# A written-out order of work, rearranged: chunked attention and a sine MLP on one core

## The chip, the core and the metric

The kernel runs on one core of one Trainium2 chip. The metric is the device time of one execution in microseconds. Three executions of the kernel before took 212.36, 212.89 and 215.1 us; the median is 212.89. One further execution was profiled: 213.36 us, of which the traced span is 211.6.

## The reference

Attention over chunks of 32 queries, for 4 batches, 8 heads, 768 positions and head size 64. A chunk's queries see 8 memory rows, the 16 positions to its left, the chunk itself and 8 positions to its right. The result, 3072 tokens of 512 numbers, goes through an MLP whose activation adds a squared sine.

```python
for c in range(nc):                       # chunks of 32
    k_full = np.concatenate([mem_k, k_ctx], axis=2)
    v_full = np.concatenate([mem_v, v_ctx], axis=2)
    scores = scale * np.matmul(q_c, k_full.transpose(0, 1, 3, 2))
    a = np.exp(scores - np.max(scores, axis=-1, keepdims=True))
    a = a / (np.sum(a, axis=-1, keepdims=True) + 1e-09)
    out[:, :, c_start:c_end] = np.matmul(a, v_full)
...
h = x @ w_in                              # 512 -> 2048
s = np.sin(alpha * h)
g = h + s * s / (alpha + 1e-09)
return g @ w_out                          # 2048 -> 512
```

## The kernel before

The program is a chain of five stages. Stage -1 is the attention of batch 0. Stage i (0 to 3) is the MLP of batch i, with the attention of batch i+1 laid into it, so that TensorE always has matmuls to do. A batch's 768 positions are eight blocks of 96 (three chunks each). Each stage's `xT` holds that batch's attention result, transposed, as the input of the next stage's first layer.

No scheduler sets the order. Each stage is a string of words, and `Stage.run` calls one method per word, in the order in which the words stand; each engine then gets its instructions in that order and works through them in order, with semaphores between engines. The words that matter here:

- `bN`, `hN`: first layer of tile N of 16 (128 hidden units), for the first and the second half of the positions, four matmuls each (L460); `h` adds the sine on ScalarE (ACT, L475). The tile holds a pair of PSUM banks.
- `qNV`, `qNA`, `qNP`: the square of tile N's sine on VectorE (DVE), ScalarE or GpSimd (POOL) (L480, L483). `gN`: `h + s*s/alpha` on DVE into `gT` (L487), which frees the pair of banks.
- `oG` opens the second layer of the stage; `fN` lets it do up to N of its 96 matmuls (L498). A finished output tile is copied to SBUF by DVE or ACT in turn (L505) and stored by SP (L508).
- `sABC`: one score group of batch i+1: the scores of blocks A, B, C (L421) and then their exponentials on ACT (L435), each block in a pair of banks. `vA`: its values (L450), normalised on DVE (L394, L395) into one of six `x_blk` buffers.
- `tA`, `TA`: block A is turned into `xT` by four TensorE transposes (L407) and a copy on DVE or ACT (L410). `cA`: the same by a transposing DMA issued by SP (L671), without TensorE.
- `kN`, `lN`, `KN`, `LN`: turns of k and q of batch 1 on TensorE and their copies. Batches 2 and 3 take k and q by rows (`R`, POOL's DMAs L232, L238, L245) and by transposing DMAs on SP (`X`, L260, L263).
- `I`, `U`, `V`, `d`: loads of `w_in`, `w_out`, v, and k or q, issued by POOL (L213, L219, L172 and L179, L155). They stand in POOL's queue between its squares. `W`: a one-element activation that has ACT load a function table.
- In stage -1, `vAB` are the values of head pair A, half B (L380), and `nA`, `yA`, `rA` make the reciprocals of pair A's sums.

TensorE, DVE, ACT and POOL meet in eight PSUM banks. `Banks` gives out, at build time, the pair that was given back longest ago; a tile's first half waits for the earlier reader of the pair's first bank, and its second half for that of the second. The single buffer of `xT` is free by the time the next batch's blocks are written, since all `b` and `h` of a stage come before its first `v`. A block by crossbar and a block by TensorE differ in these lines:

```python
def turn_x(self, a, eng):                     # t, T
    turned(x_blk, x[:, :, QW * int(a):QW * int(a) + QW], eng)
    xslots.give(x_blk)
def do_c(self, a):                            # c
    xslots.give(x_blk, 14)
    nc.sync.dma_start_transpose(x, x_blk[:].rearrange("p g e d -> p (g e d)"))
```

Of the kernel before, what the change touches and what calls it, by code (L numbers as in the profile page):

```python
# [85 lines left out]
def kernel(  # L86
# [769 lines left out]
    def const_a():  # L856
# [13 lines left out]
    ))  # L870
    for i, words in enumerate(((
# [6 lines left out]
    ),(  # L878
# [5 lines left out]
    ),(  # L884
# [5 lines left out]
    ),(  # L890
# [3 lines left out]
    ))):  # L894
        stage = Stage(i, stage.nx).run(words)
    feed.take(400)
# [29 lines left out]
```

## Time and profile before

| what | us |
|---|---|
| median of three executions | 212.89 |
| profiled execution, its own time | 213.36 |
| its traced span | 211.6 |
| TensorE matmul busy | 203.7 (96% of the span) |
| ACT busy | 144.1 (68%) |
| DVE busy | 136.6 (65%) |
| POOL busy | 101.0 (48%) |
| stage 0 and the scores and values in it | 22.8 to 73.8 |
| stage 1 | 73.8 to 120.4 |
| stage 2 | 120.4 to 166.4 |
| stage 3 and the last second layer | 166.4 to 211.6 |

All times in the profile count from the span's start. The granted TensorE clock is 1.00 in every 10 us of it. A matmul's recorded duration overlaps the next one's, so TensorE's own pace is read from the starts, that is, from a chain row's time divided by its count. A row of the chain is start, duration and what was done, with xN for N instructions in a row; a row of the timeline adds the operation's shapes and, in brackets, for how long the engine had waited and for whom.

### The profile page before, as it was taken

To read this page: it belongs to the slowest core of one execution; us is meant where nothing else is said; L and a number is where in the kernel's file an instruction comes from. 1 tells how busy PE (TensorE), PEld (TensorE's weight loads), DVE (VectorE), ACT (ScalarE), POOL (GpSimd) and SP (SyncE) were. 2 spreads that over 40 slices of the span, in tenths; PEclk is the share of its full clock that TensorE was granted. 3 is DMA by queue.
4 is the path that set the end of the run, shared out by engine and by line. 5 is a ranking of instruction groups with operands and counts; after the bars stand their busy time and mean duration, and the time that the engine had idled before them with its cause. 6 is when DMAs were issued, how large, how long until landed. Compare 5 with 4: busy or idle time off the path is not lost.

```text
span 211.6 us, 4427 instructions
## 1 busy us (share of the span) xinstructions
PE 203.7 (96%) x1701; PEld 112.6 (53%) x1701; DVE 136.6 (65%) x219; ACT 144.1 (68%) x229; POOL 101.0 (48%) x132
## 2 busy tenths in 40 slices
PE   7897999999999999999999999999999999999993
PEld 2563565655455555555456555554555565654442
DVE  6773698999362669957675669896347287864011
ACT  4699598967838579978827299878755199991110
POOL 8999608497696390019990058579300022200000
PEclk9999999999999999999999999999999999999999
DMA  6999999999999899969999239959944400000312
GB/s 172 184 155 153 208 206 204 204 155 178 171 162 108 161 138 142 163 101 118 133 232 123 71 87 133 175 104 125 173 114 114 136 3 0 0 5 8 141 51 99
DMA packets 95853, 27.02 MB, mean 128 GB/s; under 512 B 84808, under 2 KB 92376, under 8 KB 95832
## 3 DMA queue, kind: packets, MB, share of 16 engines
q0 software_dynamic: 70240, 14.43, 94.0%
q1 hardware_dynamic: 25376, 12.27, 25.0%
q8 instruction: 13, 0.21, 0.4%
q10 hardware_dynamic: 216, 0.05, 0.1%
q14 instruction: 8, 0.07, 0.1%
HBM read 29.66 MB, written 6.29 MB: 170 GB/s over the span
## 4 chain that ended last, share of the span: by engine, by line
PE 79%; DVE 7%; DMA 4%; POOL 3%; ACT 3%; issue 2%; DVEq 0%
PE ps L498 38%; PE ps L460 32%; DMA vw<-in_v_dram 4%; PE ps L450 3%; DVE gT L487 2%; PE ps L421 2%; PE ps L725 2%; DVE s L483 2%; ACT u L475 1%; ACT s L480 1%; DVE kT L298 1%; PE ps L407 1%; POOL vw L179 1%; POOL s L483 1%; POOL vw L172 1%
## 5 line engine op out<-in xcount | busy, mean ns | idle before, releaser
L498 PE MATMUL ps<-w_out_sb,gT 128*128 128x512 bf16 (+2 forms) x400 | 89.1, 371 | 0.0
L460 PE MATMUL ps<-xT,w_in_sb 128*128 128x384 bf16 x512 | 86.2, 326 | 0.6 <-DVE gT L487 0.4
L487 DVE SCALAR_TENSOR_TENSOR gT<-s,inv_alpha,ps 128x768 bf16<-128x768 f32 x64 | 63.1, 1012 | 12.3 <-ACT s L480 5.3
L475 ACT ACTIVATE u<-ps,alpha_sb 128x768 f32<-128x768 f32 x64 | 56.6, 895 | 18.5 <-PE ps L460 16.0
L460 PEld LDWEIGHTS <-w_in_sb 128*128 128x128 bf16 x512 | 49.8, 98 | 35.6 <-issue 2.4
L498 PEld LDWEIGHTS <-gT 128*128 128x128 bf16 x400 | 36.5, 98 | 37.9 <-DVE gT L487 0.2
L483 POOL TENSOR_TENSOR s<-u 128x768 f32<-128x768 f32 x11 | 17.2, 1567 | 69.2 <-ACT u L475 69.1
L435 ACT ACTIVATE pt<-ps,biasm 128x256 bf16<-128x256 f32 x72 | 27.2, 490 | 10.5 <-PE ps L421 10.5
L505 DVE COPY o_sb<-ps 128x512 f32<-128x512 f32 (+1 forms) x15 | 10.1, 678 | 28.3 <-PE ps L498 26.4
L483 DVE TENSOR_TENSOR s<-u 128x768 f32<-128x768 f32 x23 | 21.9, 953 | 7.3 <-ACT u L475 7.3
L480 ACT ACTIVATE s<-u 128x768 f32<-128x768 f32 x30 | 25.0, 841 | 0.5
L505 ACT COPY o_sb<-ps 128x512 f32<-128x512 f32 (+1 forms) x10 | 5.6, 562 | 21.6 <-PE ps L498 21.6
L395 DVE TENSOR_TENSOR x_blk<-ps,rinv 96x512 bf16<-96x512 f32 x24 | 16.5, 686 | 0.8
L172 POOL DMA_DIRECT2D vw<-in_v_dram x13 | 11.9, 913 | 5.1 <-PE ps L407 5.1
L179 POOL DMA_DIRECT2D vw<-in_v_dram x13 | 13.3, 1020 | 0.4 <-issue 0.4
L394 DVE RECIPROCAL rinv<-ps 96x8 f32<-96x8 f32 x24 | 4.7, 198 | 12.7 <-PE ps L450 12.7
L238 POOL DMA_DIRECT2D kst<-in_k_dram x16 | 11.8, 736 | 2.2 <-DMA vw<-in_v_dram 1.6
L232 POOL DMA_DIRECT2D kst<-in_k_dram x16 | 11.7, 733 | 1.4 <-DMA w_out_sb<-in_moe_w_out_dram 0.7
L245 POOL DMA_DIRECT2D q_bf<-in_q_dram x12 | 10.7, 910 | 0.0
L450 PEld LDWEIGHTS <-pt 128*128 128x128 bf16 x192 | 8.2, 97 | 4.2 <-ACT pt L435 0.3
L725 PE MATMUL ps<-zeros 128*128 128x512 bf16 x19 | 7.8, 489 | 1.3 <-DVE zeros L755 1.3
L450 PE MATMUL ps<-vw,pt 128*128 128x65 bf16 x192 | 8.9, 193 | 0.0
(89 smaller groups left out, 136.0 us busy)
## 6 DMA issues: line engine op xcount, KB each, us to landing
out_dram<-o_sb SPq DMA_DIRECT2D x23, 256.0 KB, 2.7
q_bf<-in_q_dram POOLq DMA_DIRECT2D x12, 128.0 KB, 6.6
w_in_sb<-in_moe_w_in_dram POOLq DMA_DIRECT2D x1, 1152.0 KB, 12.1
vw<-in_v_dram POOLq DMA_DIRECT2D x7, 128.0 KB, 7.2
vw<-in_v_dram POOLq DMA_DIRECT2D x8, 112.0 KB, 7.2
kst<-in_k_dram POOLq DMA_DIRECT2D x14, 64.0 KB, 4.7
kst<-in_k_dram POOLq DMA_DIRECT2D x14, 56.0 KB, 4.5
w_out_sb<-in_moe_w_out_dram POOLq DMA_DIRECT2D x2, 384.0 KB, 9.9
```

What stands on the lines that cost most here:

```text
L172: nc.gpsimd.dma_start(vw[0:64, lo:c1, 0:D], win(vflat, a, n, 64))
L179: nc.gpsimd.dma_start(vw[72:128, c0:hi, 0:D], win(vflat, base + QW * c0 + 48, hi - c0, 56))
L395: nc.vector.tensor_tensor(out=x_blk[:].rearrange("p g e d -> p e g d"), in0=otv[0:QW, :, :, 0:D], in1=rinv[:].unsqueeze(3).to_broadcast([Q ...
L435: nc.scalar.activation(pt[:, 0:H * QW].rearrange("p (g e c) -> p g e c", g=2, e=4)[:, :, :, 32 * m:32 * m + 32], sc[:, :, 0:4 * QW].rearra ...
L450: nc.tensor.matmul(otv[:, e, hp, :], pt[:, QW * i:QW * i + P], vws[b % 2][:, 2 * hp + e, j, 0:D + 1],)
L460: nc.tensor.matmul(t["hT"][:, hf, 0:HALF], w_in_sb[:, kt, P * t["ft"]:P * t["ft"] + P], t["xT"][:, kt, HALF * hf:HALF * hf + HALF], start= ...
L475: nc.scalar.activation(t["u"][:], t["hT"][:, :, 0:HALF], ACTF.Sin, scale=alpha_sb[:, ft:ft + 1])
L480: nc.scalar.activation(s2[:], u[:], ACTF.Square)
L483: e.tensor_tensor(out=s2[:], in0=u[:], in1=u[:], op=ALU.mult)
L487: nc.vector.scalar_tensor_tensor(out=gT[:, ft, :].rearrange("p (e c) -> p e c", e=2), in0=t["s2"][:], scalar=inv_alpha[:, ft:ft + 1], in1= ...
L498: nc.tensor.matmul(o[:, c0:c1], gT[:, ft, P * s:P * s + P], w_out_sb[:, ft, c0:c1], start=(ft == 0), stop=(ft == FT - 1),)
L505: copier(state["engines"][state["o"] % len(state["engines"])])(o_sb[:, c0:c1], o[:, c0:c1])
```

## The change

Only the words are rearranged; no function and no instruction's form changes. Stage -1 puts head pair 2's values ahead of pair 1's. Stages 0 and 1 each send five blocks of the next batch by crossbar instead of three (two fewer by TensorE each), stage 2 seven instead of eight (one by TensorE). The score groups are eleven instead of twelve: in stage 1 three instead of five, in stage 2 four instead of three. In stage 0 the squares of tiles 4, 9 and 15 go from DVE to POOL and that of tile 14 to ACT; in stage 1 that of tile 12 goes from POOL to DVE; in stage 3 those of tiles 6 and 10 leave ACT for DVE and POOL, and that of tile 13 goes from DVE to POOL. The other words keep their kind and shift by a few places. One line of stage -1 and the tail of stage 0, out of the table:

```diff
-        'r1 v01 v00 v11 r2 y3 I27 z1 z1 Cs v21 Cp r3 v20 z1 dm Ws v10 v30 v31 z1 '
+        'r2 v01 v00 y3 r1 r3 v21 v20 I27 z1 z1 Cs Cp v11 v10 z1 dm Ws v30 v31 z1 '
...
-        'K0A V102 f9 g14 s61 f16 m1 s70 s3 f13 v0 f3 v6 c6 f6 v3 f5 s542 T3 f10 T0 v4 f6 v2 f2 v1 '
-        'c4 c2 f7 v7 f1 T1 f3 v5 Ws T7 f8 t5 '
+        'V102 K0A f1 f9 s61 g14 f15 m1 f3 s037 f13 v6 c6 v0 f7 v3 c3 f5 c0 s4 s52 f2 f13 v1 v2 f4 '
+        'v4 c2 c4 f9 v7 f1 T1 f3 v5 T7 f5 t5 Ws '
```

What this makes of the engines' queues, at three places (lines with - stand in before, with + in the changed kernel).

POOL in stage 0, from the load of batch 1's q on. `q_bf`, `k_bf`, `w_out_sb` and `vw` are loads; `s<-u` is a square: of tile 6 in the unmarked row, of tiles 4, 7 and 9 in the added ones.

```order
 L155 DMA q_bf<-in_q_dram 128x8x384
+L483 TENSOR_TENSOR s_550<-u 128x768
 L155 DMA k_bf<-in_k_dram 128x8x384
-L219 DMA w_out_sb<-in_moe_w_out_dram 128x512 x3
+L219 DMA w_out_sb<-in_moe_w_out_dram 128x512 x2
 L483 TENSOR_TENSOR s_590<-u 128x768
+L219 DMA w_out_sb<-in_moe_w_out_dram 128x512
 L219 DMA w_out_sb<-in_moe_w_out_dram 128x2x512
-L483 TENSOR_TENSOR s_618<-u 128x768
+L483 TENSOR_TENSOR s_620<-u 128x768
 L219 DMA w_out_sb<-in_moe_w_out_dram 128x512
+L483 TENSOR_TENSOR s_647<-u 128x768
```

The square of tile 4 now stands ahead of the load of batch 1's k, that of tile 6 ahead of one more load of `w_out`, and that of tile 9 ahead of the first loads of batch 1's v. Further on in the same queue the square of tile 15 stands ahead of the remaining four loads of v.

ACT in stage 0, from the sines of tiles 2, 6, 5 and 7 (`u<-ps` x4) to the two copies of q (`qT`). The squares are those of tiles 5, 10 and 8, in this order.

```order
 L475 ACTIVATE u<-ps,alpha_sb 128x768 x4
-L480 ACTIVATE s_601<-u 128x768
+L480 ACTIVATE s_602<-u 128x768
+L475 ACTIVATE u<-ps,alpha_sb 128x768 x2
+L480 ACTIVATE s_634<-u 128x768
 L475 ACTIVATE u<-ps,alpha_sb 128x768
-L480 ACTIVATE s_634<-u 128x768
-L475 ACTIVATE u<-ps,alpha_sb 128x768 x2
-L480 ACTIVATE s_659<-u 128x768
+L480 ACTIVATE s_661<-u 128x768
 L475 ACTIVATE u<-ps,alpha_sb 128x768 x2
 L312 COPY qT_88<-ps 128x768 x2
```

Before, the sine of tile 10 was followed by its square and then by the sines of 9 and 8; now the sine of 9 comes ahead of the square of 10.

SP from the first output rows of stage 0 to stage 1's start. `out_dram` are output rows, `xT<-x_blk` blocks of batch 1 by crossbar, `kst` the memory rows of batch 2.

```order
-L508 DMA out_dram<-o_sb 128x512 x3
+L508 DMA out_dram<-o_sb 128x512 x2
+L671 DMA_TRANSPOSE xT<-x_blk_91 128x4x96
+L508 DMA out_dram<-o_sb 128x512
+L671 DMA_TRANSPOSE xT<-x_blk_93 128x4x96
 L671 DMA_TRANSPOSE xT<-x_blk_92 128x4x96
 L508 DMA out_dram<-o_sb 128x512
-L671 DMA_TRANSPOSE xT<-x_blk_94 128x4x96
 L671 DMA_TRANSPOSE xT<-x_blk_95 128x4x96
+L671 DMA_TRANSPOSE xT<-x_blk_96 128x4x96
 L508 DMA out_dram<-o_sb 128x512 x2
 L253 DMA kst<-memv_st 8x8x512
```

Blocks 6, 3, 0, 2 and 4 now go by crossbar, in this order, where blocks 6, 4 and 2 did; the last two again stand back to back, ahead of the last two output rows, but block 4 is now the last one, and block 2 was.

34 rows, old and new, of the table stage are left out of this document.

## The prediction

> **What bounds the kernel now.** I read the page first (busy shares, chain by line), then the chain in order of time, then single stretches of the timeline.
>
> ```profile
> span 211.6 us, 4427 instructions
> PE 203.7 (96%) x1701; PEld 112.6 (53%) x1701; DVE 136.6 (65%) x219; ACT 144.1 (68%) x229; POOL 101.0 (48%) x132
> ...
> PE 79%; DVE 7%; DMA 4%; POOL 3%; ACT 3%; issue 2%; DVEq 0%
> ```
>
> PE is busy for 96% of the span and is 79% of the chain that ended last. So a move on another engine is worth only the PE wait that it ends or makes. The chain shows where PE was not the limit:
>
> ```profile
> 12.06 8.03 DMA vw<-in_v_dram
> 20.23 0.51 PE ps L380 x8
> ...
> 23.21 10.54 PE ps L460 x63
> ...
> 36.52 4.08 PE ps L460 x24
> 40.62 0.91 ACT u L475
> 41.60 1.83 POOL s L483
> 43.46 1.01 DVE gT L487
> ...
> 52.19 3.56 PE ps L498 x16
> ...
> 59.27 0.24 PE ps L450 x8
> ...
> 66.08 0.17 PE ps L407 x4
> ...
> 73.80 10.44 PE ps L460 x64
> ...
> 100.05 0.45 PE ps L421 x16
> 100.49 2.91 PE ps L498 x13
> 103.41 0.62 PE ps L421 x24
> ```
>
> There are two such places: the wait for V, from 12.06 until 20.09, and batch 0's MLP from 40.62 to 52, where ACT, POOL and DVE carry the chain. From 52 on it is nearly all PE. The unit prices are there too: one first-layer matmul 10.44/64 = 0.163 us, one second-layer matmul 2.91/13 = 0.22, one block's values 0.24, one block's TensorE transposes 0.17, a score group of two blocks 0.45 and of three 0.62, so 0.17 a block and 0.11 a group.
>
> **The change part by part.** *Work taken off PE.* TensorE turned ten x blocks; now it turns seven (two less in stage 0, two less in stage 1, one more in stage 2): 3 x 0.17 = -0.51. Groups go from twelve to eleven: -0.11. Both lie on the engine that sets the end, so -0.62 holds as far as nothing new waits.
>
> *The front.* Pair 1's values waited for V; pair 2's, loaded earlier, now go first.
>
> ```profile
> 20.84 0.56 DVE L385 TENSOR_TENSOR xT<-ps,r_sb 128x384 bf16<-128x384 f32 x1 [1.18 <-PE ps L380]
> 21.67 2.42 DVE L385 TENSOR_TENSOR xT<-ps,r_sb 128x384 bf16<-128x384 f32 x5 [0.28 <-PE ps L380]
> ...
> 14.96 1.53 POOL L213 DMA_DIRECT2D w_in_sb<-in_moe_w_in_dram  x2
> ...
> w_in_sb<-in_moe_w_in_dram POOLq DMA_DIRECT2D x1, 640.0 KB, 9.3
> ...
> 22.84 3.92 PE L460 MATMUL ps<-xT,w_in_sb 128*128 128x384 bf16 x21
> ```
>
> Six multiplies of 0.48 us (2.42/5) stood behind the wait; pair 2's two leave it. The fourth of the five, which the first tile's last matmul needs, ended at 21.67 + 4 x 0.48 = 23.6; now it is third after 20.84, 22.3, so 1.3 us sooner. But the 17th matmul opens tile 4, whose columns come with the 640 KB load: issued second of the pair, at about 15.7, landed 9.3 later, 25.0. Before, that matmul stood near 25.8 (21 matmuls end by 26.7, four of them behind it). So at most 0.8 us of the head start passes this gate.
>
> *Batch 0's MLP.* Squares of tiles 4, 9 and 15 go from DVE to POOL, of 14 to ACT: four times 0.95 us off DVE, where DVE was in the chain.
>
> ```profile
> L483 DVE TENSOR_TENSOR s<-u x23: 947/951/959, 25.6 to 189.6; 128x768 f32<-128x768 f32 x23
> L483 POOL TENSOR_TENSOR s<-u x11: 1457/1463/2031, 32.3 to 180.8; 128x768 f32<-128x768 f32 x11
> ...
> 36.24 0.84 ACT L480 ACTIVATE s<-u 128x768 f32<-128x768 f32 x1
> 36.99 1.93 ACT L475 ACTIVATE u<-ps,alpha_sb 128x768 f32<-128x768 f32 x2
> ...
> 39.70 1.82 ACT L475 ACTIVATE u<-ps,alpha_sb 128x768 f32<-128x768 f32 x2
> 41.42 1.49 ACT L312 COPY qT<-ps 128x768 bf16<-128x768 bf16 x2
> ...
> 46.50 1.94 DVE L487 SCALAR_TENSOR_TENSOR gT<-s,inv_alpha,ps 128x768 bf16<-128x768 f32 x2
> ```
>
> Followed along the queues, the head start is used up here. (a) The square of tile 10 (36.24) now stands behind the sine of tile 9, which puts 0.9 us ahead of it. Begun 0.4 sooner, it still ends 0.5 later, near 37.7; tile 10's finish (1.0) ends near 38.9, and tile 13, which takes tile 10's banks, cannot start before about 39.0. It started at 39.1 before (the row 36.52 of the chain is tiles 8, 11 and 13: 36.52 + 16 x 0.163). (b) Sines 11 and 13 and the two copies of q (39.70 to 42.91) stand in the same order; tile 15 takes the banks that the copies free (the first ends near 42.2), so PE is level with before at about 42.3. (c) Tile 15's square now follows on POOL: the square of 13 ends at 43.4 (41.60 + 1.83), three weight issues of about 0.7 take it to 45.5, 1.46 more to 47.0. DVE's finish of 15 starts there, not at 46.50, and the finish of 12, whose banks two turns of k wait for, behind it: +0.5. (d) Against it, DVE drops two squares of 0.95 (15 and 14) before the first scores, and ten second-layer matmuls (2.2 us) on PE lie between those turns and the scores and cover most of (c). The stage ends between 0.4 sooner (DVE's saving counts) and 0.5 later (the wait counts, nothing covers it). Row 46.50 is the nearest, since DVE works in order, and speaks for the late end; half of it, +0.25, is my term.
>
> *Loads behind the new squares.* On POOL the square of tile 4 holds the 768 KB load of k behind it.
>
> ```profile
> 22.40 0.88 POOL L155 DMA_DIRECT2D k_bf<-in_k_dram  x1
> ...
> 41.61 0.53 PE L287 MATMUL ps<-ident,k_bf 128*64 128x128 bf16 x12
> ...
> k_bf<-in_k_dram POOLq DMA_DIRECT2D x1, 768.0 KB, 18.8
> vw<-in_v_dram POOLq DMA_DIRECT2D x7, 128.0 KB, 7.2
> ```
>
> Tile 4 opens at 25.0, takes eight matmuls (1.3), a sine (0.9) and the square (1.46): the load is issued near 29, not at 22.40. Before, it took 18.8 us to land, against 7.2 for a V load, because it lay behind the loads issued ahead of it; they cover the delay, so it lands near 41.2 either way, before PE's first turn of k at 41.61: 0. Without that cover it lands at 29 + 18.8 = 48 and PE waits 6. The V loads behind tile 15's square are issued up to 1.5 later, the last near 50 (three weight issues and four V issues of 0.7 to 0.9 from 43.4, and the square); 7.2 later is 57, and the first values stood at 59.27: 0 again.
>
> *More blocks by crossbar.* Each is 1.2 us on SP, which has the room; what counts is the last before a stage's first matmuls.
>
> ```profile
> L671 SPq DMA_TRANSPOSE xT<-x_blk x14: 1179/1199/1753, 62.0 to 164.3; - x14
> DMA to landing us min/median/max: 2.3/4.1/5.8
> ...
> 68.05 2.49 SPq L671 DMA_TRANSPOSE xT<-x_blk  x2
> ...
> 73.64 2.65 PE L460 MATMUL ps<-xT,w_in_sb 128*128 128x384 bf16 x15
> ```
>
> Before, the last of batch 1's was issued at about 69.3 and PE opened the next stage at 73.64 without an idle mark: it landed within 4.3. Now block 4 is last. From the start of its values to the second half tile, which is the first that needs it, PE has 18 second-layer matmuls (3.9), three blocks' values (0.7), three turns (0.5) and a half tile (0.65): 5.8. DVE normalises blocks 1, 2 and 4 in a row and is done with block 4 some 1.8 after that start (an estimate: two blocks of 0.9 are left by then). That leaves 4.0 for issue and landing. I take 0, by the border itself, which shows no wait at up to 4.3; the ends are 0 and 5.8 - 4.0 = 1.8.
>
> *The rest.* The table load for the sines of stage 1 now stands behind the last output copy.
>
> ```profile
> 73.66 0.59 ACT L505 COPY o_sb<-ps 128x512 f32<-128x512 f32 x1 [0.44 <-PE ps L498]
> 75.18 0.90 ACT L475 ACTIVATE u<-ps,alpha_sb 128x768 f32<-128x768 f32 x1 [0.93 <-PE ps L460]
> ...
> 99.49 1.28 ACT L738 ACT_TABLE_LOAD   x1
> ```
>
> 73.66 + 0.59 + 1.28 + 0.2 = 75.7, so the first sine is 0.55 late. Three open tiles beside it cover that: 0, at worst 0.5. In stage 3 the square of tile 6 leaves ACT for DVE, which idled there, and those of 10 and 13 go to POOL: within 0.2 either way. No other edit of stages 1 to 3 changes what PE waits for: 0, +-0.3.
>
> Sum: -0.51 - 0.11 + 0.25 = -0.37 on the profiled execution, whose own time was 213.36 us (span 211.6 and 1.76 around it). The median of the runs shown, 212.89, lies 0.47 below that one; the same difference from it gives **212.5 us**.
>
> **The rivals.** *A, the head start stays.* If the squares on POOL keep ahead of DVE, PE arrives at the first turn of k up to 0.4 sooner (41.61 against k's landing at 41.2; k is the cap), and DVE's saving ends another 0.4 of waits: -0.62 - 0.8 = -1.4, 211.5 us. For it: DVE's place in the chain from 43.46. Against: (a) to (c).
>
> *B, the crossbar comes late, slower.* At the border to stage 1 block 4 lands 5.8 after its issue instead of under 4.3: +1.8, and +1.2 at the border to stage 2, where block 7 has 0.6 more room: 212.5 + 1.8 to 3.0 = 214.3 to 215.5; a landing of 4.5 to 5 gives 213.0 to 213.5. It decides from a landing over 4.0. For it: the longest row. Against: that border's own row, and that loads from POOL are few there.
>
> *C, the two squaring engines block each other.* POOL's squares alone take 1457 ns, up to 2031 beside a DVE square, which stays at 951: the later one was held, and that was always POOL. With some five places where the two can meet, one DVE square held for 1.46 would pass to the finish behind it and to PE. Two or three such cost 2 to 4 us: 214.5 to 216.5. Against: at each meeting DVE's square became ready first.
> [...]
>
> **How the numbers follow.** Chances: forecast 0.62 (212.0 to 213.1, the bounds -0.4 and +0.5 of batch 0's MLP with the smaller ones partly against each other); A 0.17; B 0.13; C 0.05; anything else 0.03. The range 211.2 to 213.9 takes in A and the milder half of B and leaves out about 0.2. Two per cent, about what a measurement of this kernel can tell from no change, is 4.3 us: faster would need 208.6, below A; slower 217.1, which takes B and C together or the loads of k without their cover (212.5 + 6). So faster 0.01, same 0.96, slower 0.03.
>
> **What would show it.** Right: 28 matmuls at L407 instead of 40; first matmul of L460 a microsecond sooner, tile 15 at about 42.3; first scores of batch 1 at 51.5 to 52.2; no PE idle mark at the stage borders. Wrong: k or V naming PE's waits after 23 us (POOL's queue), an xT wait at a border (B), DVE squares over 1 us (C), or first scores before 51.2 (A).

## The result, and the profile after

The change makes the kernel slower: 225.94 us median (224.08 to 227.42) against 212.75 for the kernel before beside it, a ratio of 1.0598 (95% interval 1.0542 to 1.0655). The forecast was 212.5, and its range ended at 213.9. The profiled execution took 226.59 us; its span is 13.2 us longer than before's. The page, with its shares, the TensorE clock in 40 slices of 5.6 us, and the chain that ended last:

```profile
span 224.8 us, 4402 instructions
PE 209.0 (93%) x1689; PEld 113.6 (51%) x1689; DVE 134.2 (60%) x216; ACT 142.9 (64%) x225; POOL 106.1 (47%) x136
...
PEclk9999999999999999997599999998899999999999
...
PE 54%; DMA 19%; POOL 14%; SPq 4%; issue 3%; ACT 3%; DVE 2%; DVEq 0%; POOLq 0%; ACTq 0%
```

PE's part of the chain fell from 79% to 54%; DMA and POOL took it. The clock, full in every slice before, drops in two places, at about 101 to 112 and 152 to 163 us. The chain in order of time (start, us, what), first the front, then those two places:

```profile
15.71 9.55 DMA w_in_sb<-in_moe_w_in_dram
25.31 7.97 PE ps L460 x48
...
51.52 0.45 PE ps L421 x16
...
84.34 11.96 DMA vw<-in_v_dram
96.30 8.87 DMA qT<-q_bf
105.17 0.14 issue
105.31 0.82 PE ps L421 x16
106.13 5.48 PE ps L498 x13
...
147.81 7.89 DMA qT<-q_bf
155.70 0.14 issue
155.84 0.50 PE ps L421 x8
156.34 6.22 PE ps L498 x22
```

The first scores of batch 1 come at 51.52, where they were forecast (51.5 to 52.2). The loss is where stages 1 and 2 open the scores of the next batch. PE waits there for q, turned by transposing DMAs that SP issues. The waits of PE over the whole program after 60 us (total, times, longest):

```profile
PE ps L421 <- DMA qT<-q_bf: 8.6, 3, 5.6
```

What follows runs slowly: the trace has the granted clock at one half from 104.5 to 111.3 us and from 155.7 to 159.1. The 13 second-layer matmuls after the first score group took 2.91 us before (the chain row at 100.49) and take 5.48 now; 22 in stage 2 take 6.22 instead of 22 x 0.22 = 4.8. Waits 8.6, 13 slow matmuls 2.6, the slow score group of stage 1 0.4 (0.82 against 0.45), stage 2's matmuls 1.4: 13.0 of the 13.2. Windows of before and then of after (us, busy and count of PE, PEld, DVE, ACT, POOL, then the granted clock, the time of the DMA packets as a share of the 16 engines' time, which can pass 1, and GB/s):

```profile
100.00:110.00 10.00, 10.00 (x110) 5.41 (x110) 6.86 (x12) 6.51 (x17) 10.00 (x14) 1.00 2.54 183
```

```profile
100.00:110.00 10.00, 4.69 (x26) 2.11 (x27) 1.95 (x4) 2.75 (x7) 4.28 (x6) 0.72 1.63 121
```

Why q comes late stands in POOL's queue. Before, in stage 1 (a pair of rows is one V load in its two parts; L232 and L238 load rows of k for batch 3):

```profile
76.30 3.52 POOL L245 DMA_DIRECT2D q_bf<-in_q_dram  x4
94.22 1.46 POOL L483 TENSOR_TENSOR s<-u 128x768 f32<-128x768 f32 x1 [14.39 <-ACT u L475]
95.63 0.88 POOL L172 DMA_DIRECT2D vw<-in_v_dram  x1
...
99.87 0.87 POOL L179 DMA_DIRECT2D vw<-in_v_dram  x1
100.73 0.64 POOL L232 DMA_DIRECT2D kst<-in_k_dram  x1
```

And after:

```profile
76.40 3.53 POOL L245 DMA_DIRECT2D q_bf<-in_q_dram  x4
79.89 0.86 POOL L172 DMA_DIRECT2D vw<-in_v_dram  x1
...
84.34 0.87 POOL L179 DMA_DIRECT2D vw<-in_v_dram  x1
86.50 0.63 POOL L232 DMA_DIRECT2D kst<-in_k_dram  x1 [1.29 <-DMA q_bf<-in_q_dram]
```

Before, POOL stood for 14.39 us at the square of tile 12, waiting for its sine, and everything queued behind it, six V issues and the k rows of the next batch, waited too. The change gave that square to DVE. No square holds the loads now: the V loads are issued 15 to 16 us sooner and the first k row 14, and they run beside the transposing DMAs of k and q (issued from 78 to 102 us). All of them are slow together. The six V loads took 10.2 to 16.0 us to land (4.5 to 6.1 before), the transposes of k 8.3 in the median (4.7 before). By the profile, the k rows behind them waited 7.8 us in POOL's queue for V loads, and SP's queue waited 2.9 us for V loads and 3.7 for k rows before it issued transposes of q. The first scores need the fourth of q's six transposes. It was issued 2.1 us later than before (96.30 against 94.20) and landed 8.87 us after that, while PE was free from 99.7. Issue to landing of the q transposes (q's tile, 86 to 110 us; the profile has the landing of three of six before and of four after), before and after:

```profile
DMA to landing us min/median/max: 2.4/4.0/5.3
```

```profile
DMA to landing us min/median/max: 7.0/8.3/9.4
```

Stage 2 has the same in small: the two issues of the large V load (L172, L179), which stood behind the square of tile 13 and came after the last transpose of that group, now go ahead of that square and of the first q transpose. From 135 to 160 us the landing went from a median of 2.5 to 7.9:

```profile
DMA to landing us min/median/max: 2.4/2.5/2.6
```

```profile
DMA to landing us min/median/max: 7.5/7.9/7.9
```

### The profile page after: what moved, and what is told of

Read it like the earlier page. It is cut to its first block, busy times and chain, and to the rows that moved or that the text cites. A ratio compares the mean times of both kernels' runs of the same rounds, so it can differ in the third digit from the quotient of the medians.

```text
span 224.8 us, 4402 instructions
## 1 busy us (share of the span) xinstructions
PE 209.0 (93%) x1689; PEld 113.6 (51%) x1689; DVE 134.2 (60%) x216; ACT 142.9 (64%) x225; POOL 106.1 (47%) x136
## 4 chain that ended last, share of the span: by engine, by line
PE 54%; DMA 19%; POOL 14%; SPq 4%; issue 3%; ACT 3%; DVE 2%; DVEq 0%; POOLq 0%; ACTq 0%
PE ps L498 35%; PE ps L460 13%; DMA qT<-q_bf 7%; DMA vw<-in_v_dram 5%; DMA w_in_sb<-in_moe_w_in_dram 4%; POOL vw L172 4%; POOL vw L179 3%; PE ps L450 3%; PE ps L421 2%; POOL s L483 2%; SPq L260 2%; SPq L263 2%; DMA kst<-in_k_dram 2%; POOL q_bf L245 2%; ACT u L475 2%
## 5 line engine op out<-in xcount | busy, mean ns | idle before, releaser
L498 PE MATMUL ps<-w_out_sb,gT 128*128 128x512 bf16 (+2 forms) x400 | 92.8, 383 | 0.0
L498 PEld LDWEIGHTS <-gT 128*128 128x128 bf16 x400 | 37.5, 100 | 41.3 <-issue 4.9
L483 POOL TENSOR_TENSOR s<-u 128x768 f32<-128x768 f32 x15 | 23.1, 1546 | 74.3 <-ACT u L475 74.3
L483 DVE TENSOR_TENSOR s<-u 128x768 f32<-128x768 f32 x20 | 19.1, 955 | 9.8 <-ACT u L475 9.8
L480 ACT ACTIVATE s<-u 128x768 f32<-128x768 f32 x29 | 24.1, 841 | 0.7
L172 POOL DMA_DIRECT2D vw<-in_v_dram x13 | 12.5, 965 | 5.7 <-PE ps L407 5.4
L238 POOL DMA_DIRECT2D kst<-in_k_dram x16 | 11.7, 731 | 7.0 <-DMA vw<-in_v_dram 5.0
L421 PE MATMUL ps<-qT,kT 64*128 64x96 bf16 x192 | 6.5, 212 | 8.6 <-DMA qT<-q_bf 8.6
L232 POOL DMA_DIRECT2D kst<-in_k_dram x16 | 11.0, 684 | 7.0 <-DMA vw<-in_v_dram 5.1
L179 POOL DMA_DIRECT2D vw<-in_v_dram x13 | 12.4, 953 | 0.6 <-issue 0.6
L421 PEld LDWEIGHTS <-kT 64*128 64x128 bf16 x192 | 4.8, 98 | 12.9 <-issue 11.0
```

The lines of the kernel that those rows point to most:

```text
L172: nc.gpsimd.dma_start(vw[0:64, lo:c1, 0:D], win(vflat, a, n, 64))
L179: nc.gpsimd.dma_start(vw[72:128, c0:hi, 0:D], win(vflat, base + QW * c0 + 48, hi - c0, 56))
L421: nc.tensor.matmul(sc[:, e, QW * hp:QW * hp + QW], kTs[b % 2][64 * e:64 * e + 64, hp, pitch * j:pitch * j + P], qTs[b % 2][64 * e:64 * e + ...
L480: nc.scalar.activation(s2[:], u[:], ACTF.Square)
L483: e.tensor_tensor(out=s2[:], in0=u[:], in1=u[:], op=ALU.mult)
L498: nc.tensor.matmul(o[:, c0:c1], gT[:, ft, P * s:P * s + P], w_out_sb[:, ft, c0:c1], start=(ft == 0), stop=(ft == FT - 1),)
```

## The experiments

The theory: a POOL square that waits holds back the loads behind it, like a gate; where the change took the gate away, loads run beside the transposes, and q is late. Its rival: another edit of stages 1 and 2 (score groups, blocks by crossbar, DVE's load) makes q or PE late.

**One gate put back in stage 1.** The changed kernel, with tile 12's square on POOL as before:

```diff
-'... b14 h14 X6 q12V h13 V202 q13A '
+'... b14 h14 X6 q12P h13 V202 q13A '
```

> The changed kernel with one word back: the square of tile 12 in stage 1 on POOL again, in its place ahead of the last six loads of batch 2's v and of the loads of batch 3's k. Theory (the square held those loads back, and without it they collide with the crossbar transposes of q): PE's wait for qT in stage 1 (5.65 us) and the slow matmuls behind it (12 at 0.427 instead of 0.216 us, 2.5) go, stage 2's wait stays: 225.9 - 8.2 = about 217.5 us. Rival (the two more x blocks by crossbar in stages 0 and 1 are what delays q): the wait stays, 225 to 226.5. Rival (stage 2's wait is only the echo of stage 1's): both waits go, 212 to 213.

Measured: 219.32 us (218.51 to 220.37), ratio 1.0308 (1.0270 to 1.0346). No wait for q is left in stage 1; 6.6 of the 13.2 us are gone. Stage 2's is larger than it was, 4.6 us instead of 8.6 - 5.6 = 3.0, which is most of why the time is 1.8 above what was expected. The waits from 80 to 165 us:

```profile
PE ps L421 <- DMA qT<-q_bf: 4.6, 2, 3.3
```

**The other gate, in stage 2.**

```diff
-'... b12 g10 V305 q13P X3 g13 h14 '
+'... b12 g10 q13P X3 V305 g13 h14 '
```

> The changed kernel with one pair of words exchanged in stage 2: the square of tile 13 on POOL ahead of the two big loads of batch 3's v again, as before. Theory: stage 2's two waits for qT (1.4 and 1.8) and the seven slow matmuls (1.4) go, stage 1's stay: 225.9 - 4.6 = about 221.3 us. Rival (crossbar of x, or echo of stage 1): unchanged, 225 to 226.5.

Measured: 220.66 us, ratio 1.0351 (1.0317 to 1.0385). As expected, stage 2 has no wait, and stage 1 keeps its own, a microsecond longer than in the changed kernel:

```profile
PE ps L421 <- DMA qT<-q_bf: 6.6, 1, 6.6
```

**Both gates.** The two edits above together.

> The changed kernel with both: the square of tile 12 of stage 1 back on POOL, and in stage 2 the square of tile 13 ahead of the loads of v. Everything else of the change stays (pair 2 first, seventeen x blocks by crossbar, eleven score groups, the other moved squares). Theory: no wait for qT is left and the time is what was forecast for the change without this step: 212.5, in 211.5 to 213. Rival (more crossbars of x cost by themselves): 214 or more.

Measured: 212.94 us (212.68 to 214.16), ratio 1.0003 (0.9983 to 1.0022). No wait for q is left, and the q transposes of stage 1 land as before:

```profile
DMA to landing us min/median/max: 2.5/3.5/5.2
```

So the two edits carry the whole loss, and the rest of the change (the front, three blocks fewer on TensorE, one group fewer, seven squares on other engines) moves the time by no more than 0.5 us either way. The forecast's -0.37 lies at the end of that interval.

**Both edits alone, in the kernel before.**

```diff
-'... b14 h14 q12P g12 b13 h13 V202 q13A '
+'... b14 h14 q12V g12 b13 h13 V202 q13A '
...
-'... h14 b12 q13P X3 V305 h12 g13 q12V '
+'... h14 b12 V305 q13P X3 h12 g13 q12V '
```

> The kernel before with only the two edits of the POOL queue: stage 1's square of tile 12 on DVE, and stage 2's loads of batch 3's v ahead of the square of tile 13. Theory: these two alone make the whole loss: 212.8 + 12.5 = about 225, with PE waiting for qT in both stages. Rival (they matter only together with the other moved words): 213 to 218.

Measured: 227.65 us, ratio 1.0617 (1.0550 to 1.0684), an interval that overlaps the whole change's. One square and one load, moved alone, are enough for the loss. Its waits:

```profile
PE ps L421 <- DMA qT<-q_bf: 9.4, 4, 5.1
```

**Is it POOL's queue, or DVE's extra square?** Stage 2's gate is back; in stage 1 tile 12's square stays on DVE, and the next tile's goes to POOL, ahead of the V loads:

```diff
-'... X6 q12V h13 V202 q13A '
+'... X6 q12V h13 q13P V202 '
```

> Stage 2's gate is back; in stage 1 the square of tile 12 stays on DVE as in the changed kernel, and the next tile's (13) goes from ACT to POOL, ahead of the V loads. If what counts is that some POOL square holds the V and k loads back until late in the stage: 213 (212.7 to 213.8, since the gate opens about a microsecond later and ACT loses a square). If it is the engine of tile 12's square, or DVE's load beside it: 219 to 221, as with stage 2's gate alone (220.66).

Measured: 213.3 us (212.74 to 214.24), ratio 1.0026 (1.0013 to 1.0040). The next tile's square serves as a gate as well; which engine squares tile 12 makes no more than 0.4 us here (213.3 against 212.94 with both gates). POOL's row reads as before's, two microseconds later:

```profile
96.11 1.46 POOL L483 TENSOR_TENSOR s<-u 128x768 f32<-128x768 f32 x1 [16.69 <-ACT u L475]
97.52 0.89 POOL L172 DMA_DIRECT2D vw<-in_v_dram  x1
```

**Which of the loads?** Both gates are back, but the six V issues of stage 1 go ahead of the square; only the k rows stay behind it (the lines with - are those of the kernel with both gates):

```diff
-'... X6 q12P h13 V202 q13A g12 f7 ...  s42 f6 V268 f2 ...  v6 V357 f4 '
+'... X6 V202 V268 V357 q12P h13 q13A g12 f7 ...  s42 f6 f2 ...  v6 f4 '
```

> Both gates are back (stage 1's square of tile 12 on POOL, stage 2's big V loads behind the square of tile 13), but the six V loads of batch 2 are put ahead of the square of tile 12, as early as in the changed kernel; only the row loads of k for batch 3 stay behind the square. If the V loads alone slow the transposing DMAs of q: the wait of stage 1 is back whole, 212.9 + 7.7 (what the kernel with only stage 2's gate lost) = 220.6. If the row loads of k do it alone: 212.9. If it takes both together, something between, 214 to 218.

Measured: 217.35 us (216.62 to 217.76), ratio 1.0208 (1.0185 to 1.0232): 4.4 us over the kernel with both gates, of the 7.7 that stage 1's missing gate costs. The wait is 2.3 us instead of 6.6, and the slow matmuls (4.15 for 13 instead of 2.91) make up most of the rest:

```profile
95.17 6.55 DMA qT<-q_bf
101.72 0.14 issue
101.85 0.82 PE ps L421 x16
102.68 4.15 PE ps L498 x13
```

So with the V loads early and the k rows gated, over half of the loss is back. That isn't the V loads alone: with the V issues out of their way, the k rows too start sooner than before, at 95.18 instead of 100.73, beside the fourth transpose of q (95.17 to 101.72):

```profile
95.18 0.68 POOL L232 DMA_DIRECT2D kst<-in_k_dram  x1
```

The first transpose of q, issued at 90.30, took 8.0 us to land, and for the first 4.9 of them no k row of batch 3 was out. How the loss divides between V and k stays open; the k rows early and the V loads gated weren't run.

**Do the slow matmuls follow from PE's idle time?** The changed kernel, with matmuls on zeros that nobody reads ahead of the late groups:

```diff
-'... g15 s42 f6 V268 ...  f5 s24 f3 '
+'... g15 z24 s42 f6 V268 ...  f5 z16 s24 f3 '
```

> The changed kernel, with matmuls on zeros put in front of the two late score groups, whose results nobody reads: 24 in stage 1 (24 x 0.216 = 5.2 us, inside the wait of 5.65) and 16 in stage 2 (3.5 us; the waits are 3.25 together). If the second layer's slow pace of 0.427 us a matmul follows from PE's having stood idle: the waits of q stay, the slow matmuls go, 19 x 0.21 = 4.0 less, 225.9 - 4.0 = 221.9, or some tenths above where the added matmuls outlast the wait of stage 2. If the slow pace comes from the loads that run then: no gain, 226 or more.

Measured: 224.47 us (222.95 to 227.99), ratio 1.0523 (1.0468 to 1.0578). Expected was 221.9; the interval overlaps the changed kernel's, so the median settles nothing. The granted clock says more. In the changed kernel's four executions it was 0.970 to 0.977 over the span. Here it was 1.00 in two of the four, and these took 222.95 and 223.17 us, less than any of the changed kernel's four (224.08 to 227.42).

The profile is that of the longest execution (227.99, clock 0.992). In stage 1 q came even later and PE still stood idle for 2.3 us after the zeros, yet the 13 matmuls behind ran at full pace. In stage 2, where PE idled twice behind the zeros (0.4 and 1.55 us), they did not:

```profile
107.09 0.52 PE ps L421 x16
107.61 2.91 PE ps L498 x13
...
157.08 0.35 PE ps L421 x8
157.43 6.54 PE ps L498 x22
```

The slow pace does not go with the loads. The first window below is stage 1 of this run, where the matmuls kept full pace at clock 1.00 while the DMA engines moved 129 GB/s. The second is stage 2 of the kernel with stage 1's gate alone, where 16 matmuls filled 5 us at clock 0.68 and no DMA packet was started:

```profile
105.00:110.00 5.00, 2.91 (x28) 1.53 (x28) 0.74 (x2) 2.30 (x6) 1.43 (x2) 1.00 2.08 129
```

```profile
150.00:155.00 5.00, 4.95 (x16) 2.00 (x16) 0.00 (x0) 0.55 (x2) 0.00 (x0) 0.68 0.00 0
```

So the slow pace goes with the granted clock: in the changed kernel the second-layer matmuls start every 0.427 us while it is 0.50, and every 0.216 from 111.3 and 159.1 us on, where it is 1.00 again. In stages 1 and 2 of every profile it falls only where PE waits for q. The matmuls on zeros did not bring q sooner: in stage 1 it landed at 107.05 us, and at 105.17 in the changed kernel.

**The front undone.** Both gates back, and stage -1's last line as before the change:

```diff
-'r2 v01 v00 y3 r1 r3 v21 v20 I27 z1 z1 Cs Cp v11 v10 z1 dm Ws v30 v31 z1 '
+'r1 v01 v00 v11 r2 y3 I27 z1 z1 Cs v21 Cp r3 v20 z1 dm Ws v10 v30 v31 z1 '
```

> Both gates are back, and the line of stage -1 is as before the change (pair 1's values ahead of pair 2's); stages 0 to 3 are as changed. If the head start of the front is used up by the first scores, as forecast: 212.9, the same as with both gates (212.94), within 0.4. If the front alone carries a gain: 213.7 to 214.3. If the front costs: under 212.5.

Measured: 213.03 us, ratio 1.0019 (1.0004 to 1.0033), against 1.0003 (0.9983 to 1.0022) with the new front. The head start is worth at most some tenths of a microsecond, and the two can't be told apart. A gain of 0.8 or more from the front, as the expectation put it for rival A, is not there.

## Why the prediction was wrong

**The step that failed** is the last sentence on the parts of the change: "No other edit of stages 1 to 3 changes what PE waits for: 0, +-0.3". It measured +13.2: 7.7 in stage 1 (the kernel with only stage 2's gate against the one with both) and 6.4 in stage 2 (219.32 - 212.94), which together slightly overstate it. Under it lies a one-sided look at POOL's queue. "Loads behind the new squares" asked what each *added* square holds back, and answered 0 for k and for V, which was right: neither is among PE's waits after 23 us. The load of k, issued at 29.22 instead of 22.40, landed at 41.4 us (41.2 before), and PE's weight loads waited 0.2 us for it. What a *removed* square lets go was not asked, although the trace of before shows it: 14.39 us idle at one square, six V issues and the k rows behind it, the transposes of q running meanwhile. The exchange of tile 13's square with the large V load in stage 2 isn't named at all; it is among the words that "shift by a few places". What came of it had no term either: the transposes of q took 4.3 and 5.4 us longer to land in the median, and at PE's waits the clock stood at one half for 6.83 and 3.41 us, 10.2 together.

**"Work taken off PE", -0.62.** 28 matmuls at L407 instead of 40, as forecast:

```profile
L407 PE MATMUL ps<-ident,x_blk 96*128 96x96 bf16 x28 | 2.2, 205 | 0.0
```

What it is worth in time is under what the runs tell apart: the kernel with both gates stands level with before (1.0003), within an interval of -0.4 to +0.5.

**"The front" and "Batch 0's MLP".** The wait for the 640 KB load is as forecast. The 17th matmul of the first layer waits for it, forecast for 25.0, and goes on at 25.31:

```profile
22.18 2.77 PE L460 MATMUL ps<-xT,w_in_sb 128*128 128x384 bf16 x16 [0.21 <-DMA w_in_sb<-in_moe_w_in_dram]
25.31 1.96 PE L460 MATMUL ps<-xT,w_in_sb 128*128 128x384 bf16 x11 [0.36 <-DMA w_in_sb<-in_moe_w_in_dram]
```

The head start itself can't be read from these traces. The first layer starts here at 22.18, before at 22.84. But two other runs with the front of before started it at 21.60 (both edits alone in the kernel before) and 21.94 (the front undone), and the seven with the new front lie between 21.52 and 22.18. The first scores scatter as much: 50.55 to 51.67 with the old front, 50.95 to 51.46 with the new, all by the start of the first matmul. That the chain has 51.52, where the forecast put it, is therefore partly luck, the sign for rival A ("first scores before 51.2") tells nothing, and whether the term of +0.25 was right stays open. The times alone bound it: with both gates back, all terms but the failed one add up to between -0.4 and +0.5.

**Rival A** would have given 211.5 with both gates back; measured was 212.94.

**"More blocks by crossbar", 0.** Right, and rival B did not occur: `xT` is named in none of PE's waits after 60 us. B looked for trouble with the crossbar, but for the wrong tile: it asked when the *last x block* is issued, while what went wrong was how long the *q transposes* take once other loads run beside them. Its own argument against, "loads from POOL are few there", was the place to ask whether that still holds after the change.

**Rival C.** Nor did C:

```profile
L483 POOL TENSOR_TENSOR s<-u 128x768 f32<-128x768 f32 x15 | 23.1, 1546 | 74.3 <-ACT u L475 74.3
L483 DVE TENSOR_TENSOR s<-u 128x768 f32<-128x768 f32 x20 | 19.1, 955 | 9.8 <-ACT u L475 9.8
```

One DVE square held for 1.4 us would have put the mean of 20 at 1.02; it is 955 ns, within the 947 to 959 of before. POOL's, 1457 alone, are again the ones that stretch, up to 1798 (2031 before). No run shows a DVE square held for the length of POOL's: in the traces of before and after the longest took 959 and 989 ns, so the 1.46 in C's sum was the author's estimate.

**The chances.** Slower had 0.03. All rivals on that side were mishaps of steps that the text had priced; the edit that decided was put into the remainder, with a width of 0.3 that no row carried.

## What to carry to other kernels

In an in-order queue that both computes and issues DMAs, as POOL's is here, a waiting compute instruction is also a gate on the transfers behind it (14.39 us at one square, with six V issues and the k rows behind it): before it is moved to another engine, list what stands behind it, when that will now start, and which latency-critical DMA runs at that time. Price the removal of a wait with the same care as the addition of one, also when the engine is off the critical path. A wait on TensorE can cost more than its length: here 5.6 us of waiting brought 2.6 us of slow matmuls, with the granted clock at 0.50 from 104.5 to 111.3 us.

## What was unexpected of the hardware

**A transposing DMA lands two to three times later beside loads.** The q transposes took 4.0 us to land in stage 1 before (median), and 8.3 after; in stage 2 2.5, and 7.9. With both gates back it was 3.5 and 2.4. What slowed them beside the loads (an engine's time, memory or something else) no run separated.

**The granted clock fell at waits that aren't long, and not at all of them.** The slow matmuls start every 0.427 us instead of 0.216, half the pace, and the trace has the granted clock at 0.50 there: in the changed kernel from 104.47 to 111.29 us, at the end of the wait of 5.58, and from 155.67 to 159.08, at the end of waits of 1.34 and 1.67. One wait of 2.3 us (the kernel with only its V loads early) was followed by about six slow matmuls (13 in 4.15 us instead of 2.91; the clock of 100 to 105 us is 0.67). But 2.3 us in stage 1 of the kernel with the zeros were followed by none (13 in 2.91 us, clock 1.00), nor were two waits of 3.0 us together in stage 2 of the kernel before with both gates removed (clock 1.00 from 150 to 160 us). So the length of a wait alone doesn't say whether the clock falls; what does, no run shows.
